# A Fourier-filter and maxout kernel: the opening's row fix, last products, last tile and first transforms rearranged, and one read split

## The chip, the cores and the metric

The kernel runs on one core of a Trainium2 chip. A core has TensorE (matrix products), VectorE, ScalarE and GpSimd (elementwise work), SyncE, which issues transfers here, and 16 DMA engines that all queues share. The metric is the time of one execution on the device in microseconds; smaller is better. Values come from the median of repeated executions; the profile is of one execution.

In the profile's rows PE is TensorE, PEld its weight loads, DVE VectorE, ACT ScalarE, POOL GpSimd and SPq the transfer queue of SyncE. L12 is line 12 of the kernel before.

## The reference

A global filter in the frequency domain along the sequence, and a two-branch maximum network over each token.

```python
# x: (8, 3072, 256); filt_r, filt_i: (1537, 256); w1, w2: (256, 1024); w_out: (1024, 256)
X = np.fft.rfft(x, axis=1)
Y = X * (filt_r + 1j * filt_i)[None, :, :]
y = np.fft.irfft(Y, n=3072, axis=1).reshape(24576, 256)
h = np.maximum(y @ w1, y @ w2)
out = h @ w_out
```

## The kernel before

**The transform.** The 3072 positions are split as 96 x 32. A transform of length 96 (stage 1), one of length 32 with the twiddle factors (stage 2), the product with the filter, and the two inverse stages (3 and 4) are all matrix products with tables of sines that the kernel makes itself. `C1` is the table of stage 1, `U` that of stage 2 (24 units `u` of 64 columns), `VP` and `VQ` those of stage 3, `G1` that of stage 4. `F` holds the filter in 12 x 2 slices. Stages 2, product and 3 run over six pairs of units, `v` = 0 to 5: `s2(b, v)` makes two tiles `px`, `product` makes two tiles `pq` of 128x1024 from them and `F`, and `s3` (for batch 0 `s3t`) makes `pz` from these.

**The network.** `max(a, b) = relu(a - b) + b`, so the kernel takes `Wd = w1 - w2` and `M = w2 @ w_out`. Tokens go in 64 tiles `tt` of 384, eight to a batch: `moe_h(tt, j)` (j = 0 to 7, L476) makes `ph` with `Wd` and ScalarE or VectorE takes its relu into `gt`; `moe_o(tt, ...)` (L519) accumulates `po` from `M` with `y` and from `Wo` with `gt`, and VectorE and a transfer on GpSimd's queue bring it out.

**The order.** Everything runs in the order in which it is written (`manual_schedule`), engine by engine. There are two parts.

*The opening*, L621 to L718, takes batch 0 through its transform on the chip alone, and prepares the weights:

- Tables: `table_c` (L180), `tables_u`, `sines_u`, `table_g` (L251), `table_v` and `put_v` (L256, L273). Stage 1 is `s1t` (L554), its turn is `t1` (L566).
- The filter: GpSimd's queue issues `load_f`; `put_fz` writes 32 rows, `double_f` copies half of `F` (VectorE for the first eight slices, L128), and `fix_f` (L144) writes one row of one slice.
- [...] For v = 5 `shared_product` (L394) gives three quarters of the second one to VectorE and one quarter to GpSimd.
- `s3t(v, pq)` (L577) is 32 products of 64x64 columns into two PSUM tiles, led by products with the constant `W1` (128x512, L581) whose result nobody reads; its two tiles are then written to `zT` by ScalarE, for v = 4 and 5 by ScalarE and VectorE.
- `t2(c, engines)` (L599) turns four of `zT`'s 32 columns back with eight transposes into `pr`, and the engines named copy it to `zr`. `s4(tt)` (L454) makes `y` of a token tile from it and `G1`: two tiles `py`, one evicted by ScalarE, one by VectorE.
- `spin(n)` (L615) is n products with `W1` in between, again unread.
- Behind the products GpSimd's queue does, in this order: `load_x(1, 2, 2)`, `load_wo`, `prep_wd(0)`, two more `load_x`, `prep_wd(1)` to `(3)` (a quarter of `Wd` each, L298), `cast_w2` twice (half of `w2b` each, L291) and `table_ct`. Quarter q of `Wd` serves j = 2q and 2q + 1. `prep_t(0)` (L300) transposes the first half of `w2b`, `prep_m` makes `M`.

*The stream*, L777 on, runs 64 steps per batch, step = 8 i + j. At each step it calls `moe_h`, some of `moe_o` of the tile before, and what the tables `mid` and `todo` hold for that step: the transform of the next batch. For batch 1 that is `f1(1, c)` (L323, c = 0 to 15; the first four stand in the opening): a product with `C1` into `pa`, an eviction to `at` by ScalarE or VectorE, and for each odd c a store to the DRAM tile `ad`. `f1_read(1)` (L340) reads it back as `bt` in three pieces (units 0-4, 4-12, 12-24) at step 13. `visit(1, n)` at steps 25, 28, 31, 35, 38, 42 and 46 does `s3(1, n-1)`, `s2(1, n)`, stage 1 of batch 2 for some quads, and the products. Batch 2's input comes by `load_xf(2, c)` (L91, SyncE's queue, three buffers `XF`) and `fold(2, c)` (GpSimd, L101) at steps listed in `plan_f2`.

[...] A tile that is made waits until the tile that used its bank before has been read.

Of the kernel before, what the change touches and what calls it, by code (L numbers as in the profile page):

```python
# [15 lines left out]
D = 256  # L16
HID = 1024
NP = 96
# [9 lines left out]
def kernel(  # L28
# [115 lines left out]
    def fix_f():  # L144
        V.tensor_copy(F[32:33, 0, 0, 0], FZ[32:33, 0])

# [8 lines left out]
    cid = init.tile([128, 128], FP32)  # L155

    hv = init.tile([128, 2, 1], FP32)
    load_x(0, 0, 1)
# [33 lines left out]

    def table_ct():
# [127 lines left out]
    at_ = {}  # L321

    def f1(b, c, engine):  # L323
# [4 lines left out]
        at = at_[b]  # L328
        pa = ps.tile([96, 2, D], FP32, tag="ps", name="pa")
        TE.matmul(pa, C1, xb[b, c // 2][:, 2 * (c % 2):2 * (c % 2) + 2], start=True, stop=True)  # L330
        o_ = at[0:96, 2 * (c % 4):2 * (c % 4) + 2]
        if engine is V:
            V.tensor_copy(o_, pa)
        else:
            S.activation(o_, pa, AF.Copy)
        if c % 2 == 1:
            m0 = 2 * (c % 4) - 2
            nc.sync.dma_start(out=ad[b][:, 2 * c - 2:2 * c + 2], in_=at[0:96, m0:m0 + 4])

    def f1_read(b):  # L340
        bt[b] = bpool.tile([128, NU, D], BF16, tag="bt", name="bt")
        src = ad[b].rearrange("(u q) m d -> (q m) u d", q=4)
        for u0, u1 in ((0, 4), (4, 12), (12, NU)):
            nc.sync.dma_start(out=bt[b][:, u0:u1], in_=src[:, u0:u1])

# [42 lines left out]
    def product(E, v, s, px, pool=None):  # L388
        pq = (pool or pqpool).tile([128, 2, 2, D], BF16, tag="pq", name="pq")
        E.tensor_tensor(pq, px.rearrange("p (o i) d -> p o i d", o=1).to_broadcast([128, 2, 2, D]),  # L390
                        F[:, :, 2 * v:2 * v + 2, s], OP.mult)
        return pq

    def shared_product(v, s, px, xs_, pool):  # L394
        pq = pool.tile([128, 2, 2, D], BF16, tag="pq", name="pq")
        V.tensor_tensor(pq[:, 0], px, F[:, 0, 2 * v:2 * v + 2, s], OP.mult)
        V.tensor_tensor(pq[:, 1, 0], px[:, 0], F[:, 1, 2 * v, s], OP.mult)
        G.tensor_tensor(pq[:, 1, 1], xs_[:, 1], F[:, 1, 2 * v + 1, s], OP.mult)
        return pq
# [177 lines left out]
    def s3t(v, pq):  # L577
        pool, tag = (ps, "ps") if v % 2 else (pso, "po")
        pz = [pool.tile([128, 2, 2, 2, 2, NM], FP32, tag=tag, name="pt%d" % g) for g in range(2)]
        for _ in range(2 if v == 1 else 1):  # L580
            TE.matmul(pz[0].rearrange("p i s r c m -> p (i s r c m)"), W1[:, 0:128], W1, start=True, stop=True)  # L581
        for i in range(2):
            for s in range(2):
                for dc in range(2):
                    for q, tab in enumerate((VP, VQ)):
                        for g in range(2):
                            TE.matmul(pz[g][:, i, s, :, dc], pq[s][64 * g:64 * g + 64, q, i, 128 * dc:128 * dc + 128],  # L587
                                      tab[64 * g:64 * g + 64, 2 * v + i, s].rearrange("p (r m) -> p r m", r=2),
                                      start=(q == 0), stop=(q == 1))
        zv = zT.rearrange("p c m (w g) q -> p w g (c m) q", g=2)  # L590
        for g in range(2):
            o_ = zv[:, 2 * v:2 * v + 2, g]
            i_ = pz[g].rearrange("p i s r c m -> p i (c m) (s r)")
            if v >= 4 and g == 1:
                V.tensor_copy(o_, i_)
            else:
                S.activation(o_, i_, AF.Copy)

    def t2(c, engines):  # L599
# [3 lines left out]
        for k, engine in enumerate(engines):  # L603
            pr = ps.tile([96, n, D], BF16, tag="ps", name="pr")
            m0 = 4 * c + n * k
            for m in range(n):
                for dc in range(2):
                    TE.transpose(pr[:, m, 128 * dc:128 * dc + 128], zT[:, dc, m0 + m].rearrange("p u q -> p (u q)"),  # L608
                                 I128)
# [29 lines left out]
    bt[0] = bpool.tile([128, NU, D], BF16, tag="bt", name="bt")  # L639
    zT = bpool.tile([128, 2, NM, NU, 4], BF16, tag="bt", name="zT")  # L640
    for n in range(6):
# [44 lines left out]
    pxs[5] = s2(0, 5)  # L686
    stage_x(5)
    for v in (2, 3):
# [140 lines left out]
```

## Time and profile before

| what | value |
|---|---|
| median of 3 runs | 498.68 us (496.98, 498.87, 498.68) |
| the profiled execution | 498.64 us |
| its span, first to last instruction | 496.8 us |
| mean granted TensorE clock | 0.989 |
| busy: TensorE, VectorE, ScalarE, GpSimd | 483.8, 335.4, 320.4, 258.7 us |
| HBM traffic | 203 GB/s over the span |

A row of the timeline gives the start, the time, engine and line, operation, output <- inputs, shapes and the count of instructions merged; in square brackets stands the idle time before it and what ended it. A row of the chain gives start, time, engine, tile and line. A row of stretches gives the stretch, its length, the busy time of PE, PEld, DVE, ACT and POOL with counts (PE alone where it was asked for TensorE), the granted clock, the DMA engines' busy share and GB/s. Ends of matrix products are modelled: they are pipelined, so one of 512 columns shows 0.38 us but the next can start earlier.

### The profile page before, as it was taken

The page shows a single profiled execution, that of the slowest core. Times are in us where ns is not written, and L with a number is a line of the kernel's source. Part 1 is how long each engine was busy: PE and PEld are TensorE (multiplying, and loading weights), DVE is VectorE, ACT ScalarE, POOL GpSimd, SP SyncE. Part 2 cuts the span into 40 slices and gives each one's busy share as a digit, 9 for nine tenths or more (in the row PEclk, how much of TensorE's full clock was granted, in tenths as well). Part 3 has the DMA queues.
Part 4 walks back from the last instruction along what each step waited for, and adds up shares of the span by engine and source line. Part 5 has one row for each costly group of instructions (what it writes and reads, how often), then busy time and mean ns, then how long its engine had stood idle before and what let it go on. Part 6 is the DMA issues. An engine that isn't in the chain of part 4 may idle for free.

```text
span 496.8 us, 14137 instructions
## 1 busy us (share of the span) xinstructions
PE 483.8 (97%) x5759; PEld 353.5 (71%) x5759; DVE 335.4 (68%) x535; ACT 320.4 (64%) x667; POOL 258.7 (52%) x342
## 2 busy tenths in 40 slices
PE   7699999999999999999999999999999999999997
PEld 3457777777777777777777777776777777777775
DVE  7886788468855688467855688457873688556542
ACT  5777478667775677576866668665766656464442
POOL 8694868318466594528646295536842212222220
PEclk9879999999999999999999999999999999999999
DMA  8989988996789867896789977897776834531112
GB/s 128 161 242 224 259 269 260 284 234 190 204 266 221 216 210 223 249 225 174 231 257 227 183 244 211 257 215 168 227 231 175 181 104 129 157 120 66 64 64 86
DMA packets 76626, 97.30 MB, mean 196 GB/s; under 512 B 7985, under 2 KB 54354, under 8 KB 75186
## 3 DMA queue, kind: packets, MB, share of 16 engines
q1 hardware_dynamic: 63218, 66.71, 52.1%
q0 software_dynamic: 13200, 29.60, 21.4%
q8 instruction: 45, 0.74, 0.7%
q14 instruction: 19, 0.16, 0.1%
q10 hardware_dynamic: 144, 0.09, 0.1%
HBM read 53.87 MB, written 47.19 MB: 203 GB/s over the span
## 4 chain that ended last, share of the span: by engine, by line
PE 92%; DMA 3%; ACT 2%; POOL 1%; issue 1%; DVE 0%; SPq 0%; POOLq 0%
PE po L536 34%; PE ph L482 33%; PE po L534 8%; PE pz L408 5%; PE pc L443 3%; PE px L384 2%; PE pa L355 2%; DMA xb<-in_x_dram 2%; DMA zr<-zd 1%; PE pt L587 1%; DMA zd<-zt 1%; PE pr L608 1%; POOL xb L89 1%; PE pt L581 1%; PE pa L330 1%
## 5 line engine op out<-in xcount | busy, mean ns | idle before, releaser
L486 ACT ACTIVATE gt<-ph 128x384 bf16<-128x384 f32 x357 | 175.7, 496 | 138.8 <-PE ph L482 136.2
L536 PE MATMUL po<-Wo,gt 128*128 128x256 bf16 x1528 | 262.7, 273 | 1.2 <-issue 1.2
L536 PEld LDWEIGHTS <-gt 128*128 128x128 bf16 x1528 | 144.7, 98 | 68.1 <-issue 13.5
L495 POOL DMA_DIRECT2D out_dram<-ot x186 | 103.1, 558 | 154.7 <-DVE ot L547 138.7
L390 DVE TENSOR_TENSOR pq<-px,F 128x1024 bf16<-128x1024 f32 x91 | 106.9, 1218 | 25.7 <-PE px L384 25.4
L484 DVE TENSOR_SCALAR gt<-ph 128x384 bf16<-128x384 f32 x155 | 83.6, 551 | 53.5 <-PE ph L482 47.1
L482 PEld LDWEIGHTS <-Wd 128*128 128x128 bf16 x1024 | 99.6, 98 | 13.7 <-issue 0.3
L104 POOL TENSOR_TENSOR xb<-XF 128x512 bf16<-128x512 f32 x48 | 61.3, 1277 | 66.9 <-DMA XF<-in_x_dram 31.7
L547 DVE TENSOR_SCALAR ot<-po 128x512 f32<-128x512 f32 x83 | 57.0, 686 | 35.0 <-PE po L536 33.1
L105 POOL TENSOR_TENSOR xb<-XF 128x512 bf16<-128x512 f32 x48 | 61.1, 1274 | 0.0
L359 ACT ACTIVATE at<-pa 128x512 bf16<-128x512 f32 x96 | 51.8, 611 | 3.4 <-PE pa L355 3.3
L412 ACT ACTIVATE zt<-pz 128x512 bf16<-128x512 f32 x84 | 45.6, 594 | 5.7 <-PE pz L408 1.9
L448 ACT ACTIVATE ce<-pc 128x384 f32<-128x384 f32 x56 | 23.7, 490 | 6.7 <-PE pc L443 6.0
L408 PE MATMUL pz<-pq,VP 64*64 64x256 bf16 x336 | 22.2, 281 | 0.0
L384 PE MATMUL px<-bt,U 64*64 64x256 bf16 x384 | 20.4, 283 | 1.2 <-ACT VQ L279 0.7
L408 PE MATMUL pz<-pq,VQ 64*64 64x256 bf16 x336 | 21.1, 269 | 0.0
L408 PEld LDWEIGHTS <-VP 64*64 64x64 bf16 x336 | 10.0, 105 | 13.3 <-issue 12.7
L355 PE MATMUL pa<-xb,CT 64*64 64x512 bf16 x192 | 18.0, 377 | 0.0
L443 PEld LDWEIGHTS <-zr 48*128 48x128 bf16 x896 | 13.1, 93 | 4.8 <-issue 4.4
L443 PE MATMUL pc<-G,zr 48*128 48x48 bf16 x896 | 15.4, 180 | 0.3 <-DMA zr<-zd 0.3
L384 PEld LDWEIGHTS <-U 64*64 64x64 bf16 x384 | 10.6, 109 | 3.9 <-issue 3.6
L618 PE MATMUL pd<-W 128*128 128x512 bf16 x28 | 9.2, 437 | 1.5 <-DVE zero L150 1.5
(383 smaller groups left out, 632.1 us busy)
## 6 DMA issues: line engine op xcount, KB each, us to landing
out_dram<-ot POOLq DMA_DIRECT2D x186, 128.0 KB, 3.8
XF<-in_x_dram SPq DMA_DIRECT2D x96, 192.0 KB
ad<-at SPq DMA_DIRECT2D x56, 192.0 KB
zd<-zt SPq DMA_DIRECT2D x42, 256.0 KB
zr<-zd SPq DMA_DIRECT2D x56, 192.0 KB
bt<-ad SPq DMA_DIRECT2D x13, 768.0 KB
WS<-in_moe_w_dram SPq DMA_DIRECT2D x4, 512.0 KB
xb<-in_x_dram POOLq DMA_DIRECT2D x8, 192.0 KB, 5.6
```

What stands on the lines that cost most here:

```text
L104: G.tensor_tensor(t_[:, 0], f[:, 0], f[:, 1], OP.add)
L105: G.tensor_tensor(t_[:, 1], f[:, 0], f[:, 1], OP.subtract)
L359: S.activation(at[:, m0:m0 + 2], pa[g], AF.Copy)
L390: E.tensor_tensor(pq, px.rearrange("p (o i) d -> p o i d", o=1).to_broadcast([128, 2, 2, D]), F[:, :, 2 * v:2 * v + 2, s], OP.mult)
L408: TE.matmul(pz[g][64 * s:64 * s + 64, i], tab[64 * g:64 * g + 64, 2 * v + i, s], pq[s][64 * g:64 * g + 64, q, i], start=(q == 0), stop=(q ...
L412: S.activation(zt[:, :, g], pz[g], AF.Copy)
L482: TE.matmul(ph, Wd[:, dc, 128 * j:128 * j + 128], y_[:, dc], start=(dc == 0), stop=(dc == 1))
L484: V.tensor_scalar(gt[tt][:, j], ph, 0.0, None, OP.max)
L486: S.activation(gt[tt][:, j], ph, AF.Relu)
L495: E.dma_start(out=dst, in_=ot[tt // 2][:, 3 * (tt % 2) + c])
L536: TE.matmul(p_, g_[:, n - 2, blk], Wo[:, n - 2], start=(e == 0), stop=(e == 9))
L547: V.tensor_scalar(ot[tt // 2][:, e - 1:e + 1], po[q // 2 % 2], SCALE, None, OP.mult)
```

## The change

- `fix_f` runs on GpSimd in place of VectorE, at the same place of the program.
- `shared_product` and `stage_x(5)` are gone; VectorE makes both products of v = 5 whole.
- `zT` has another order of its axes, in eight groups `o` of four columns. To suit it, `G1` is made from a second sine table `CP`, which holds `C1`'s columns in another order, and `s3t` and `t2` address their tiles accordingly. For v = 5 each of the two PSUM tiles is written to `zT` in two parts: group 0 first, then groups 1 to 7.
- The unread products: `s3t` is led by 3, 4, 2, 2, 3 and 0 of them for v = 0 to 5 (before: 1, 2, 1, 1, 1, 1), and a new function `busy(n)` puts 2 behind each of `s2(0, 1)` and `s2(0, 0)`, 3 behind `table_v(0, 1)`, 9 behind `sines_u(1)` and 2 behind the last `put_v`. They write to a tile of `pso`. The two `spin(1)` ahead of the stream become `fill` of 1, 1 and 2.
- `f1` is cut into `f1_in` (the product) and `f1_out` (eviction and store). The products of c = 0 to 3 of batch 1 stand between the steps of the opening's end; the evictions of c = 0 and 1 come after `s4(0)`, those of c = 2 and 3 at step 0 of the stream.
- In batch 0 the three pieces of `f1_read` are issued at steps 13, 14 and 15; `load_xf(2, 2)` and `(2, 3)` move from steps 10 and 12 to 13 and 14 (behind that step's piece), their folds from 16 and 20 to 19 and 22.

```diff
     def fix_f():
-        V.tensor_copy(F[32:33, 0, 0, 0], FZ[32:33, 0])
+        G.tensor_copy(F[32:33, 0, 0, 0], FZ[32:33, 0])
...
+        S.activation(CP.rearrange("p (g w c) -> p g w c", g=2, c=4),
+                     uc.rearrange("p (w g s) r -> p g w (s r)", g=2, s=2), AF.Sin, bias=zero[0:NP], scale=TWO_PI)
...
-        TE.matmul(pg, C1, I128[0:NP, 0:NP], start=True, stop=True)
+        TE.matmul(pg, CP, I128[0:NP, 0:NP], start=True, stop=True)
...
     def f1(b, c, engine):
+        f1_in(b, c)
+        f1_out(b, c, engine)
+
+    def f1_in(b, c):
+        pas[c] = ps.tile([96, 2, D], FP32, tag="ps", name="pa")
+        TE.matmul(pas[c], C1, xb[b, c // 2][:, 2 * (c % 2):2 * (c % 2) + 2], start=True, stop=True)
+
+    def f1_out(b, c, engine):
...
-    def f1_read(b):
-        bt[b] = bpool.tile([128, NU, D], BF16, tag="bt", name="bt")
+    def f1_read(b, u0, u1):
+        if u0 == 0:
+            bt[b] = bpool.tile([128, NU, D], BF16, tag="bt", name="bt")
         src = ad[b].rearrange("(u q) m d -> (q m) u d", q=4)
-        for u0, u1 in ((0, 4), (4, 12), (12, NU)):
-            nc.sync.dma_start(out=bt[b][:, u0:u1], in_=src[:, u0:u1])
+        nc.sync.dma_start(out=bt[b][:, u0:u1], in_=src[:, u0:u1])
...
     def s3t(v, pq):
...
-        for _ in range(2 if v == 1 else 1):
-            TE.matmul(pz[0].rearrange("p i s r c m -> p (i s r c m)"), W1[:, 0:128], W1, start=True, stop=True)
+        for _ in range((3, 4, 2, 2, 3, 0)[v]):
+            TE.matmul(pz[0].rearrange("p o i s r c m -> p (o i s r c m)"), W1[:, 0:128], W1, start=True, stop=True)
...
-        for g in range(2):
-            o_ = zv[:, 2 * v:2 * v + 2, g]
-            i_ = pz[g].rearrange("p i s r c m -> p i (c m) (s r)")
-            if v >= 4 and g == 1:
-                V.tensor_copy(o_, i_)
-            else:
-                S.activation(o_, i_, AF.Copy)
+        for o0, o1 in ((0, 1), (1, 8)) if v == 5 else ((0, 8),):
+            for g in range(2):
+                o_ = zT[:, o0:o1, :, :, g, 2 * v:2 * v + 2].rearrange("p o c m w q -> p o (c m) (w q)")
+                i_ = pz[g][:, o0:o1].rearrange("p o i s r c m -> p o (c m) (i s r)")
+                if v >= 4 and g == 1:
+                    V.tensor_copy(o_, i_)
+                else:
+                    S.activation(o_, i_, AF.Copy)
...
     def products(v):
         pool = pq0 if v > 2 else pqpool
         pq = [product(V, v, 0, pxs[v][0], pool)]
-        if v == 5:
-            pq.append(shared_product(v, 1, pxs[v][1], xs[v], pool))
-        else:
-            pq.append(product(G, v, 1, xs[v], pool) if v in POOLED else product(V, v, 1, pxs[v][1], pool))
+        pq.append(product(G, v, 1, xs[v], pool) if v in POOLED else product(V, v, 1, pxs[v][1], pool))
         return pq

+    def busy(n):
+        pd = pso.tile([128, 512], FP32, tag="po", name="pd")
+        for _ in range(n):
+            TE.matmul(pd, W1[:, 0:128], W1, start=True, stop=True)
+
     pqs = {}
-    pxs = {v: s2(0, v) for v in (1, 0)}
+    pxs = {}
+    for v in (1, 0):
+        pxs[v] = s2(0, v)
+        busy(2)
     stage_x(0)
     put_v(0, 1, table_v(0, 1))
+    busy(3)
     pxs[2] = s2(0, 2)
     stage_x(2)
     sines_u(1)
+    busy(9)
     put_v(1, 0, table_v(1, 0))
     pxs[3] = s2(0, 3)
     stage_x(3)
     put_v(1, 1, table_v(1, 1))
+    busy(2)
...
     pxs[5] = s2(0, 5)
-    stage_x(5)
...
-    f1(1, 0, S)
-    spin(1)
+    f1_in(1, 0)
+    fill(1)
     t2(0, (V, S))
-    f1(1, 1, V)
-    spin(1)
+    f1_in(1, 1)
+    f1_in(1, 2)
+    fill(1)
     s4(0)
-    f1(1, 2, S)
-    f1(1, 3, V)
+    f1_in(1, 3)
+    f1_out(1, 0, S)
+    f1_out(1, 1, V)
+    fill(2)
...
-        plan(b, read, f1_read, nb)
+        for k, (u0, u1) in enumerate(((0, 4), (4, 12), (12, NU))):
+            plan(b, read + k, f1_read, nb, u0, u1)
...
+    plan(0, 0, f1_out, 1, 2, S)
+    plan(0, 0, f1_out, 1, 3, V)
     plan_f1(0, 1, (5, 6, 7, 7, 9, 9, 10, 10, 11, 11, 12, 12), 13)
     plan_f2(0, (25, 28, 31, 35, 38, 42, 46), ((0,), (), (1,), (2,), (3,), (4,), (5, 6)),
-            (8, 8, 10, 12, 17, 20, 24, 28), (10, 13, 16, 20, 24, 27, 30, 33))
+            (8, 8, 13, 14, 17, 20, 24, 28), (10, 13, 19, 22, 24, 27, 30, 33))
```

More of the change, by code (lines that the diff above doesn't have):

```diff
@@ L155 @@
     cid = init.tile([128, 128], FP32)
+    CP = init.tile([NP, 96], BF16)
     hv = init.tile([128, 2, 1], FP32)
@@ L321 @@
     at_ = {}
+    pas = {}
     def f1(b, c, engine):
+        f1_in(b, c)
[4 more added lines that the diff above has]
+    def f1_out(b, c, engine):
         if c == 0:
@@ L327, in f1 @@
             at_[b] = apool.tile([128, 8, D], BF16, tag="at", name="at")
-        at = at_[b]
-        pa = ps.tile([96, 2, D], FP32, tag="ps", name="pa")
-        TE.matmul(pa, C1, xb[b, c // 2][:, 2 * (c % 2):2 * (c % 2) + 2], start=True, stop=True)
+        at, pa = at_[b], pas.pop(c)
         o_ = at[0:96, 2 * (c % 4):2 * (c % 4) + 2]
@@ L391, in product @@
                         F[:, :, 2 * v:2 * v + 2, s], OP.mult)
[L392 to L398, printed above, removed]
         return pq
@@ L578, in s3t @@
         pool, tag = (ps, "ps") if v % 2 else (pso, "po")
-        pz = [pool.tile([128, 2, 2, 2, 2, NM], FP32, tag=tag, name="pt%d" % g) for g in range(2)]
-        for _ in range(2 if v == 1 else 1):
-            TE.matmul(pz[0].rearrange("p i s r c m -> p (i s r c m)"), W1[:, 0:128], W1, start=True, stop=True)
+        pz = [pool.tile([128, 8, 2, 2, 2, 2, 4], FP32, tag=tag, name="pt%d" % g) for g in range(2)]
+        for _ in range((3, 4, 2, 2, 3, 0)[v]):
+            TE.matmul(pz[0].rearrange("p o i s r c m -> p (o i s r c m)"), W1[:, 0:128], W1, start=True, stop=True)
         for i in range(2):
@@ L586, in s3t @@
                         for g in range(2):
[L587 to L588 removed]
+                            TE.matmul(pz[g][:, :, i, s, :, dc].rearrange("p o r m -> p r o m"),
+                                      pq[s][64 * g:64 * g + 64, q, i, 128 * dc:128 * dc + 128],
+                                      tab[64 * g:64 * g + 64, 2 * v + i, s].rearrange("p (r o m) -> p r o m", r=2, m=4),
                                       start=(q == 0), stop=(q == 1))
[L590 to L597 removed]
+        for o0, o1 in ((0, 1), (1, 8)) if v == 5 else ((0, 8),):
[6 more added lines that the diff above has]
+                    S.activation(o_, i_, AF.Copy)
     def t2(c, engines):
@@ L607, in t2 @@
                 for dc in range(2):
-                    TE.transpose(pr[:, m, 128 * dc:128 * dc + 128], zT[:, dc, m0 + m].rearrange("p u q -> p (u q)"),
+                    TE.transpose(pr[:, m, 128 * dc:128 * dc + 128],
+                                 zT[:, (m0 + m) // 4, dc, (m0 + m) % 4].rearrange("p g w q -> p (g w q)"),
                                  I128)
@@ L639 @@
     bt[0] = bpool.tile([128, NU, D], BF16, tag="bt", name="bt")
-    zT = bpool.tile([128, 2, NM, NU, 4], BF16, tag="bt", name="zT")
+    zT = bpool.tile([128, 8, 2, 4, 2, NW, 4], BF16, tag="bt", name="zT")
     for n in range(6):
@@ L710, with fill @@
     gpool = ctx.enter_context(tc.tile_pool(name="gpool", bufs=2))
-    f1(1, 0, S)
-    spin(1)
+    pd = pso.tile([128, 512], FP32, tag="po", name="pd")
+    def fill(n):
+        for _ in range(n):
+            TE.matmul(pd, W1[:, 0:128], W1, start=True, stop=True)
+    f1_in(1, 0)
+    fill(1)
     t2(0, (V, S))
-    f1(1, 1, V)
-    spin(1)
+    f1_in(1, 1)
+    f1_in(1, 2)
+    fill(1)
     s4(0)
-    f1(1, 2, S)
-    f1(1, 3, V)
+    f1_in(1, 3)
+    f1_out(1, 0, S)
+    f1_out(1, 1, V)
+    fill(2)
     todo = {}
```

## The prediction

> **What bounds the kernel now.** I read the page first, then the busy time by stretches, the chain of waits, and the timeline of each engine for the first 66 us, where every edit lies. PE is TensorE, DVE VectorE, ACT ScalarE, POOL GpSimd.
>
> ```profile
> PE 483.8 (97%) x5759; PEld 353.5 (71%) x5759; DVE 335.4 (68%) x535; ACT 320.4 (64%) x667; POOL 258.7 (52%) x342
> ...
> 38.00:45.00 7.00, 7.00 (x77) 5.27 (x76) 6.10 (x11) 5.56 (x11) 5.08 (x8) 1.00 1.13 206
> 38.00:98.50 60.50, 60.50 (x660) 45.09 (x660) 43.40 (x65) 41.58 (x86) 39.65 (x46) 1.00 0.93 260
> ```
>
> TensorE is busy in every microsecond from 38 to 98.5 (the busy time behind the stretch's length), and for 97% of the whole span. Whatever the opening saves reaches the end only if this stream starts earlier and still finds its inputs. The stream's first product is at 37.73. So two questions decide: by how much does 37.73 move, and what then arrives too late?
>
> The opening's own limit is in the chain of waits:
>
> ```profile
> 26.04 0.97 PE pt L581 x2
> ...
> 28.54 0.54 PE pt L581
> 29.08 1.01 PE pt L587 x30
> 30.10 0.59 ACT zT L597
> ...
> 33.22 0.58 PE pt L587 x32
> 34.11 0.62 PE pt L587 x32
> 34.76 0.70 DVE zT L595
> 35.59 0.63 PE pr L608 x8
> ```
>
> One `s3t` takes 1.01 us early and 0.58 us late, because the clock differs. I laid windows of 3.41 us on the clock's edges (the last three columns: clock, DMA share, GB/s):
>
> ```profile
> 7.64:11.05 3.41, 2.62 (x27) 1.00 1.05 172
> ...
> 17.88:21.29 3.41, 2.31 (x95) 1.00 0.92 123
> 21.29:24.70 3.41, 1.39 (x39) 0.50 0.70 146
> 24.70:28.12 3.42, 3.12 (x93) 0.50 0.56 165
> 28.12:31.53 3.41, 3.30 (x62) 0.50 1.06 289
> 31.53:34.94 3.41, 3.41 (x131) 1.00 1.03 321
> ```
>
> The half clock lasts 10.24 us, three such windows. It begins behind a window with 2.31 us of busy TensorE, while 2.62 had kept the full clock.
>
> **The change, part by part.** First the row fix and the last product pair:
>
> ```profile
> 18.11 0.49 POOL L122 DMA_DIRECT2D F<-in_filt_r_dram  x1 [0.34 <-DMA F<-in_filt_r_dram]
> ...
> 19.82 2.40 POOL L122 DMA_DIRECT2D F<-in_filt_i_dram  x2
> 23.43 2.12 POOL L390 TENSOR_TENSOR pq<-xs,F 128x1024 bf16<-128x1024 f32 x1 [1.20 <-DVE F L128]
> ...
> 26.07 6.30 POOL L390 TENSOR_TENSOR pq<-xs,F 128x1024 bf16<-128x1024 f32 x3
> 32.34 0.66 POOL L398 TENSOR_TENSOR pq<-xs,F 128x256 bf16<-128x256 f32 x1
> 32.95 0.56 POOL L89 DMA_DIRECT2D xb<-in_x_dram  x1
> 33.51 0.93 POOL L294 DMA_DIRECT2D Wo<-in_moe_w_out_dram  x1
> ...
> 36.72 3.74 POOL L298 TENSOR_TENSOR Wd<-WS 128x512 bf16<-128x512 f32 x3
> 40.40 2.01 POOL L291 CAST w2b<-WS 128x1024 bf16<-128x1024 f32 x2
> ```
>
> ```profile
> 18.49 4.76 DVE L128 COPY F<-F 32x4096 bf16<-32x4096 bf16 x4
> 23.28 0.28 DVE L145 CAST F<-XF 1x256 bf16<-1x256 f32 x1
> 23.76 8.13 DVE L390 TENSOR_TENSOR pq<-px,F 128x1024 bf16<-128x1024 f32 x7 [0.19 <-DVE F L145]
> ...
> 32.40 0.41 DVE L397 TENSOR_TENSOR pq<-px,F 128x256 bf16<-128x256 f32 x1
> ```
>
> ```profile
> L142 POOL CAST F<-XF x2: 520/562/605, 7.6 to 8.2; 32x256 bf16<-32x256 f32 x2
> ```
>
> VectorE loses the fix, so its products start at 23.28 and not 23.76; eight whole ones at 8.13/7 = 1.16 us end at 23.28 + 9.29 = 32.57. Before, the shared form ended at 32.81. Gain there: 0.24.
>
> GpSimd loses the shared quarter: 32.95 - 32.34 = 0.61 us. It gains the fix, 0.56 us by L142 (same 256 columns). It can start when the last filter issue ends, 22.22, inside an idle stretch that ends at 23.43: bound 0 us. If it has to let VectorE's copies end first (18.49 + 4.76 = 23.25), it ends at 23.81 and delays the first product by 0.38 (0.42 with L142's longest). I take 0.38: the two issues at 19.82 took 1.20 each where the one at 18.11 took 0.49, and 1.20 is the pitch of VectorE's copies (4.76/4 = 1.19), so GpSimd's work under these copies ends with them. Behind the fix stand all of GpSimd's products, loads and weight preparations. Everything from L89 at 32.95 on therefore moves earlier by 0.61 - 0.38 = 0.23 us (bounds 0.19 and 0.61).
>
> [...]
>
> The fills on TensorE: `busy` puts 2, 2, 3, 9 and 2 products of 512 columns into the stretches 18 to 26, and `s3t` goes from 1, 2, 1, 1, 1, 1 to 3, 4, 2, 2, 3, 0 (v = 0 to 5). Their aim shows in the windows: 17.88 to 21.29 rises from 2.31 by up to the seven short fills, above 2.62, and the clock should stay at 1.00 until 38. At full clock a fill costs at most 0.90 - 0.58 = 0.32 (the pitch 33.22 to 34.11 less one `s3t`). The last two reuse a buffer of the second VQ table, so they wait until ScalarE has evicted it; behind them stand `s3t(1)` and `s2(4)`, which VectorE needs for its sixth product at 23.28 + 5 x 1.16 = 29.1. `s2(4)` ended at 28.54; four more fills at 0.32 add 1.3, and the full clock takes off 0.43 (one `s3t`) and 0.33 (two fills at 0.32 for 0.97): 29.1, just in time.
>
> `s3t(4)` cannot end before GpSimd's last product, 32.37 + 0.38 = 32.75. With two `s3t` of 0.58 that gives 33.9, or 34.2 where the three fills are still in the way; I take 34.05. Before it was 34.11 + 0.62 = 34.73, so 0.68 is gained. The last tile's first part has an eighth of the columns: between 0.28 us (L145) and 0.70 (the whole tile); I take 0.3, as it is small, and gain 0.4. The second part then sits on ScalarE and VectorE ahead of the evictions of `t2(0)`, but their inputs need another 0.63 us on TensorE (L608), which covers it. The early `f1_in` and late `f1_out` move the four evictions (0.6 to 0.7 us each) behind the first `y`; nothing waits for them before step 4. Sum: the first product of the stream comes 0.68 + 0.4 = 1.1 us earlier, at about 36.6 (bounds 0.5 and 1.4). The second sine table, the order of `zT` and `G1`, and `stage_x(5)` dropped are ScalarE work with gaps around it: 0.
>
> Now what it meets:
>
> ```profile
> 37.73 0.89 PE L482 MATMUL ph<-y__998,Wd 128*128 128x384 bf16 x4
> ...
> 40.77 0.49 PE L482 MATMUL ph<-y__998,Wd 128*128 128x384 bf16 x2
> ...
> 41.64 0.61 PE L305 MATMUL pt<-I,w2b 128*128 128x128 bf16 x8
> ...
> 44.19 0.60 PE L536 MATMUL po<-Wo,gt 128*128 128x256 bf16 x4
> ```
>
> ```profile
> DMA to landing us min/median/max: 10.6/10.6/10.6
> ```
>
> (the last is the one transfer of Wo, L294.) The product at 40.77 needs the last quarter of Wd, ready at 36.72 + 3.74 = 40.46: slack 0.31. The transposes at 41.64 need the first half of w2b, ready at 40.40 + 2.01/2 = 41.41: slack 0.23. The product at 44.19 needs Wo, landed at 33.51 + 10.6 = 44.1: slack 0.1. None of these moves with TensorE; all move with GpSimd, by 0.23. So TensorE starts 1.1 early, waits, and is ahead by at most 0.54 at 40.77, 0.46 at 41.64 and 0.33 at 44.19. From there on it is dense. **Gain: 0.3 us.** Bounds: 0.1 (Wo lands no earlier, since the DMA engines are loaded: share 1.13 in 38 to 45) and 0.7 (0.61 + 0.1).
>
> Batch 0's read in pieces:
>
> ```profile
> 57.57 1.96 SPq L344 DMA_DIRECT2D bt<-ad  x3
> ...
> 65.05 0.41 PE L384 MATMUL px<-bt,U 64*64 64x256 bf16 x8
> ...
> 57.50:64.50 7.00, 7.00 (x77) 5.10 (x73) 5.25 (x8) 4.87 (x10) 6.97 (x9) 1.00 0.90 259
> ```
>
> The second piece now stands on SP behind the XF load of tile 2, and the third behind tile 3; both loads come later and leave the stores ahead of them alone. From 57.57, piece one (0.26 MB), that load (0.52 MB) and piece two (0.52 MB) are 1.3 MB; at the 259 GB/s of this stretch 5.0 us, so it lands at 62.6, before 65.05 - 0.3. Cost 0, and nothing to gain, as TensorE waited for nothing here. If the cover is gone, `s2(1,1)` and all behind it wait. Loads 5 and 6 of XF now wait for later folds, and behind them on SP stands the first store of `zd` (step 28), which is read back from step 39 on.
>
> **The sum.** The profiled execution took 498.64 us, span 496.8, so 1.8 lies around it; it agrees with the median of the three runs, 498.68. 498.64 - 0.3 = **498.3 us**.
>
> **The rivals.** *The whole opening arrives.* If GpSimd's chain were not the gate, all 1.1 would stay: 497.5. For it: POOL has idle time ahead of 23.43. Against it: three separate due times with slacks of 0.1 to 0.31. *Nothing arrives*: Wo lands where it did, 498.5.
>
> *The clock stays at half and the fills cost.* Place: TensorE from 26 to 34.7. At half clock a fill takes 0.49 (0.97 for two); two more in `busy`, two more in `s3t(1)` are 1.9 us before `s2(4)`, and five net ones follow at 0.32 (1.6 us). Against that, `s3t(0)` slips behind 31.53 and saves 0.4, and TensorE had a wait of 0.6 to spare (L597 at 30.10). `s3t(5)` ends 2.5 late; the split gives back 0.4: the stream starts 2.1 late with nothing left to absorb it, 498.64 + 2.1 = 500.7. It decides if the window 17.88 to 21.29 stays under about 2.6 us busy. For it: 3.12 us in 24.70 to 28.12 did not bring the full clock back, and where the windows fall may differ by execution. Against it: the fills close most of the 1.1 us of gaps there.
>
> [...]
>
> *Piece two comes late*: at 150 GB/s instead of 259, 1.3 MB take 8.7 us, to 66.3, 1.5 after its due time: 498.3 + 1.5 = 499.8. Against it: the rate of the row above, with the same kinds of transfer in it.
>
> **The numbers.** Forecast 0.57, whole opening 0.13, nothing arrives 0.11, half clock 0.10, late piece 0.06, something else 0.03. The runs before spread from 496.98 to 498.87; one row may tell why:
>
> ```profile
> 336.35 0.28 PE L536 MATMUL po<-Wo,gt 128*128 128x256 bf16 x1 [1.23 <-issue]
> ```
>
> This stop has no cause in the trace; an execution without it would be 1.2 us shorter. So the range goes from 498.3 - 0.5 - 1.2 = 496.6 up to 499.8, short of the half-clock case. [...] Faster 0.05 (a median without the stop and with the whole opening), slower 0.05, same 0.90.
>
> **What would show it.** Right: clock 1.00 from 18 to 38; first GpSimd product at 23.8; first stream product near 36.6; TensorE idle 0.3 to 0.8 us in all ahead of Wd, w2b or Wo between 38 and 44; L536 first at 43.9. Wrong: L536 first near 43.1, clock 0.50 anywhere after 21, TensorE idle at bt near 65, or a span over 498.

## The result and the profile after

| | before | changed |
|---|---|---|
| median | 498.10 us (22 runs, 496.63 to 499.04) | **499.14 us** (22 runs, 497.37 to 503.12) |
| profiled execution | 498.64 us, span 496.8 | 503.12 us, span 501.3 |
| ratio to before | | **1.003** (95%: 1.0019 to 1.0041) |

The changed kernel is slower by 1.04 us where 0.3 us of gain was forecast. Two more measurements of the same kernel gave 1.004 (1.001 to 1.007) and 1.0035 (1.0018 to 1.0052). The profiled execution is the longest of its 22: what it shows is real, but larger than in most. Line numbers are now the changed kernel's: L672 is `busy`, L585 the unread products of `s3t`, L591 its own products, L395 `s2`, L401 `product`, L658 ScalarE's copies of `px` to `xs`, from which GpSimd's products are made, L602 and L600 the copies to `zT`, L486 `moe_h`, L540 `moe_o`.

**The clock.** Stretches, TensorE only: length, PE busy, granted clock, DMA share, GB/s. First the kernel before, then the changed one.

```profile
18.00:38.00 20.00, 16.00 (x419) 0.74 0.87 203
38.00:98.50 60.50, 60.50 (x660) 1.00 0.93 260
98.50:125.00 26.50, 26.50 (x337) 1.00 0.89 214
318.00:345.00 27.00, 25.50 (x291) 1.00 0.90 198
```

```profile
18.00:38.00 20.00, 17.93 (x438) 1.00 0.84 201
38.00:98.50 60.50, 60.29 (x656) 1.00 0.93 235
98.50:125.00 26.50, 24.22 (x286) 0.94 0.89 212
318.00:345.00 27.00, 27.00 (x311) 1.00 1.00 238
```

The unread products did hold the full clock through the opening (1.00 for 0.74). The loss is 2.28 us of idle TensorE and a stretch of half clock between 98.5 and 125. The last row holds a gain that the forecast had only as an end of its range: the stop near 335 is gone.

**The opening.** Timelines of the changed kernel: TensorE (rows of the second tables and of `s3t`'s own products left out, but one), VectorE, GpSimd.

```profile
22.56 2.12 PE L672 MATMUL pd<-W 128*128 128x512 bf16 x9
...
27.27 0.59 PE L672 MATMUL pd<-W 128*128 128x512 bf16 x2 [0.67 <-ACT VQ L282]
27.70 1.02 PE L585 MATMUL pt<-W 128*128 128x512 bf16 x4
28.66 0.20 PE L591 MATMUL pt<-VP,pq 64*128 64x64 bf16 x2
...
29.23 0.29 PE L395 MATMUL px<-bt,U 64*64 64x256 bf16 x1
29.98 0.41 PE L395 MATMUL px<-bt,U 64*64 64x256 bf16 x7 [0.46 <-ACT zT L602]
30.32 0.82 PE L585 MATMUL pt<-W 128*128 128x512 bf16 x3
...
31.64 0.41 PE L395 MATMUL px<-bt,U 64*64 64x256 bf16 x8
```

```profile
23.67 5.75 DVE L401 TENSOR_TENSOR pq<-px,F 128x1024 bf16<-128x1024 f32 x5
30.42 1.22 DVE L401 TENSOR_TENSOR pq<-px,F 128x1024 bf16<-128x1024 f32 x1 [1.00 <-DMA xb<-in_x_dram]
32.10 2.36 DVE L401 TENSOR_TENSOR pq<-px,F 128x1024 bf16<-128x1024 f32 x2 [0.46 <-PE px L395]
```

```profile
20.14 2.41 POOL L122 DMA_DIRECT2D F<-in_filt_i_dram  x2
22.59 1.23 POOL L145 CAST F<-XF 1x256 bf16<-1x256 f32 x1
23.91 2.13 POOL L401 TENSOR_TENSOR pq<-xs,F 128x1024 bf16<-128x1024 f32 x1
...
31.13 2.13 POOL L401 TENSOR_TENSOR pq<-xs,F 128x1024 bf16<-128x1024 f32 x1 [0.36 <-ACT xs L658]
```

The last two of `busy` wait 0.67 us for ScalarE, four more follow, and `s3t(1)` begins its own work only at 28.66. Behind it `s2(4)` starts at 29.23, but its second product runs only at 29.98, right behind ScalarE's first copy to `zT` (0.46 us of idle time, 0.75 us between two products that stand 0.003 us apart in the kernel before), and it ends at 30.39. Why `s2(4)` has to wait for that copy the rows don't say. VectorE's sixth product starts at 30.42: that is its true releaser, though the bracket names a transfer long done. Its seventh starts at 32.10, right behind `s2(5)` (31.64 + 0.41). VectorE, which was to run without a break to 32.57, ends at 34.46.

**Batch 0.** Timelines of the changed kernel: SyncE's queue, then TensorE at the read-back of `zd`; last the same queue in the kernel before.

```profile
62.65 9.43 SPq L94 DMA_DIRECT2D XF<-in_x_dram  x6
72.12 0.43 SPq L417 DMA_DIRECT2D zd<-zt  x1
...
93.71 4.62 SPq L387 DMA_DIRECT2D zr<-zd  x4
...
99.42 3.10 SPq L387 DMA_DIRECT2D zr<-zd  x2
```

```profile
101.27 0.18 PE L447 MATMUL pc<-G,zr 48*128 48x48 bf16 x1 [0.61 <-DMA zr<-zd]
103.11 1.12 PE L447 MATMUL pc<-G,zr 48*128 48x48 bf16 x47 [1.66 <-DMA zr<-zd]
```

```profile
59.64 5.13 SPq L94 DMA_DIRECT2D XF<-in_x_dram  x6
66.39 0.38 SPq L413 DMA_DIRECT2D zd<-zt  x1
...
89.56 3.24 SPq L376 DMA_DIRECT2D zr<-zd  x4
93.86 1.62 SPq L376 DMA_DIRECT2D zr<-zd  x2
```

Six load issues hold the queue for 9.43 us in place of 5.13, the store of `zd` behind them starts 5.73 us later, and the last `zr` reads are issued 5.56 us later, while the stream itself was only some 2 us late. TensorE waits for them 0.61 + 1.66 us, and a window at half clock follows (103.0 to 106.4). The trace shows the chain: `load_xf(2, 2)` and `(2, 3)` now stand behind the read's first and second piece and are issued from 58.22 on (before: 51.01 to 55.27), their folds start at 64.69 and 68.77 (before: 57.56 and 61.13) behind idle waits of 4.67 and 1.59 us for these loads, and the six issues wait for the folds.

```profile
64.69 1.26 POOL L104 TENSOR_TENSOR xb<-XF 128x512 bf16<-128x512 f32 x1 [4.67 <-DMA XF<-in_x_dram]
...
68.77 1.27 POOL L104 TENSOR_TENSOR xb<-XF 128x512 bf16<-128x512 f32 x1 [1.59 <-DMA XF<-in_x_dram]
```

**The ledger.** Start of the same `ph` product in the two traces: the first 37.73 to 39.25 (+1.52, of which 0.31 is there at the first transpose of stage 1), the 17th 42.97 to 44.83 (+1.86), the 121st +2.11, the 161st, behind the `zr` wait and the half clock, +6.04; then two stops that only the kernel before has, near 326 and 335, take back 1.8, a wait for `zr` near 388 that only the changed kernel has loses 0.4, and the last `ph` product is at 493.72 for 489.23 (+4.49).

### The profile page after: what moved, and what is told of

Read it like the earlier page. It is cut to its first block, busy times and chain, and to the rows that moved or that the text cites. A ratio compares the mean times of both kernels' runs of the same rounds, so it can differ in the third digit from the quotient of the medians.

```text
span 501.3 us, 14191 instructions
## 1 busy us (share of the span) xinstructions
PE 489.8 (98%) x5786; PEld 356.1 (71%) x5786; DVE 335.3 (67%) x534; ACT 320.4 (64%) x668; POOL 258.8 (52%) x342
## 4 chain that ended last, share of the span: by engine, by line
PE 90%; DMA 5%; ACT 1%; POOL 1%; DVE 1%; SPq 0%; issue 0%; POOLq 0%; DVEq 0%; ACTq 0%
PE po L540 33%; PE ph L486 31%; PE po L538 8%; PE pz L412 5%; PE pc L447 3%; DMA zr<-zd 2%; PE px L395 2%; PE pa L366 2%; DMA xb<-in_x_dram 2%; DMA zd<-zt 1%; PE pd L672 1%; POOL xb L89 1%; PE pt L585 1%; PE pt L591 1%; PE pa L334 1%; ACT at L370 1%
## 5 line engine op out<-in xcount | busy, mean ns | idle before, releaser
L540 PE MATMUL po<-Wo,gt 128*128 128x256 bf16 x1528 | 263.2, 273 | 0.0
L540 PEld LDWEIGHTS <-gt 128*128 128x128 bf16 x1528 | 144.9, 98 | 67.1 <-issue 12.5
L401 DVE TENSOR_TENSOR pq<-px,F 128x1024 bf16<-128x1024 f32 x92 | 108.2, 1218 | 27.2 <-PE px L395 25.9
L486 PEld LDWEIGHTS <-Wd 128*128 128x128 bf16 x1024 | 99.8, 98 | 14.0 <-issue 0.2
L395 PE MATMUL px<-bt,U 64*64 64x256 bf16 x384 | 19.9, 272 | 0.5 <-ACT zT L602 0.5
L395 PEld LDWEIGHTS <-U 64*64 64x64 bf16 x384 | 10.4, 106 | 4.1 <-issue 4.0
L549 DVE COPY ot<-po 128x512 f32<-128x512 f32 x12 | 8.2, 684 | 4.2 <-PE po L540 4.2
```

Of the source, the lines that this page charges most:

```text
L486: TE.matmul(ph, Wd[:, dc, 128 * j:128 * j + 128], y_[:, dc], start=(dc == 0), stop=(dc == 1))
L540: TE.matmul(p_, g_[:, n - 2, blk], Wo[:, n - 2], start=(e == 0), stop=(e == 9))
```

## The experiments

Two loss sites, so the question was which of them the medians carry, and what in each. The theories, by the letters that the expectations use: **A**: the unread products stand on TensorE's path and delay `s2(4)`, `s2(5)` and with them VectorE. **B**: the later loads and folds hold SyncE's queue, so that `zd` and `zr` come late. **C**: the moved `f1` evictions and the divided last tile cost by themselves. **D**: the full clock is worth more than the unread products cost. **E**: the read of `bt` in three pieces is late by itself. **F**: the stop near 335 depends only on how many instructions stand ahead of it. **G**: the unread products cost only together with the rest of the new opening.

"Opening" below is the time from the first transpose of stage 1 to the start of the stream's 17th `ph` product, "stream" from there to the last `ph` product, both from the profiled execution. The first loses what happens ahead of the transposes, which differs by up to 1.4 us between executions. Openings with a star hold a wait of 2.2 to 4.1 us of VectorE for the second half of the filter, which landed late in those executions.

| run | median us | before, same chip | ratio (95%) | opening | stream |
|---|---|---|---|---|---|
| before | 498.10 | | | 27.83 | 446.26 |
| changed | 499.14 | 498.10 | 1.003 (1.0019 to 1.0041) | 29.38 | 448.89 |
| changed, 2nd | 499.45 | 498.04 | 1.004 (1.001 to 1.007) | 30.34* | 448.58 |
| changed, 3rd | 498.95 | 497.77 | 1.0035 (1.0018 to 1.0052) | 29.43 | 445.63 |
| batch 0 undone | 498.38 | 497.98 | 1.0007 (0.9996 to 1.0018) | 29.18 | 444.47 |
| the same, 2nd | 498.47 | 497.77 | 1.0015 (1.0002 to 1.0028) | 29.22 | 444.79 |
| pieces kept | 498.62 | 498.04 | 1.0012 (0.9995 to 1.0029) | 29.41 | 444.34 |
| batch 0 alone | 498.51 | 497.98 | 1.0009 (0.9996 to 1.0022) | 27.97 | 446.06 |
| late unread ones out | 497.58 | 497.98 | 0.9994 (0.9976 to 1.0011) | 28.45 | 444.62 |
| unread ones as before | 498.66 | 497.98 | 1.0016 (0.9996 to 1.0036) | 29.32* | 445.17 |
| unread ones in waits | **497.14** | 498.04 | 0.9986 (0.9966 to 1.0005) | 28.11 | 444.40 |
| fewer, one eviction later | **497.14** | 498.12 | 0.9984 (0.9964 to 1.0004) | 27.69 | 445.39 |
| unread ones in before | 497.85 | 498.12 | 0.9994 (0.9978 to 1.0011) | 29.13* | 444.37 |
| before, 28 more products | 498.24 | 498.04 | 1.0003 (0.9983 to 1.0023) | 29.77* | 444.30 |

### Batch 0: undone, alone, and its two halves apart

Undone, in the changed kernel (and in the next four experiments on the opening too):

```diff
-            plan(b, read + k, f1_read, nb, u0, u1)
+            plan(b, read, f1_read, nb, u0, u1)
...
-            (8, 8, 13, 14, 17, 20, 24, 28), (10, 13, 19, 22, 24, 27, 30, 33))
+            (8, 8, 10, 12, 17, 20, 24, 28), (10, 13, 16, 20, 24, 27, 30, 33))
```

> The opening as changed; the read in one step and the loads and folds of batch 0 as before the change. Theory A (the unread products stand on TensorE's path in the opening): the first ph stays at 39.0 to 39.3 us, and the time stays 1.0 us over before (ratio 1.002). Theory B (the loads and folds moved in batch 0 make zr of batch 1 late): the long executions above 500.5 us vanish, TensorE no longer waits for zr near 100 us, and if B were all, the ratio is 1.000.

Alone: the kernel before with this edit the other way round.

> The kernel before with only the read in pieces and the moved loads and folds. Theory A: ratio 1.000, first ph at 37.7. Theory B: the last zr read of batch 1 is issued near 98 us where it was at 93.9, TensorE waits 0.5 to 2.5 us for it near 99 in some executions, ratio 1.001 to 1.003 with a tail above 500 us.

Pieces kept: the changed kernel with the second line of the diff only (loads and folds back, reads still at steps 13, 14 and 15).

> The changed kernel with the loads and folds of tiles 2 and 3 back at steps 10, 12, 16 and 20; the read stays in three steps. Theory B (SP's queue stands behind folds that became later, and with it the zd stores and zr reads): the last zr read is issued no later than 1.5 us after its place of before relative to the first ph, no wait for zr near 100, ratio to before as with all of batch 0 undone, 1.0007 +- 0.001. Rival E (the read in pieces itself is late): the wait near 100 stays, ratio 1.002 or more.

Beside this one the changed kernel ran again on the same chip:

> The changed kernel itself once more, for a second profile. Theory B: TensorE waits 0.4 us or more for zr near 100 us here too, the last zr read of batch 1 is issued on SP 60 us or more after the first ph (before: 93.9 - 37.7 = 56.1). If the wait of the first profile was an accident: no wait over 0.2 us there.

And last both kernels in five rounds on one chip:

> The changed kernel once more, five rounds, on one chip with the same kernel less its batch 0 edit (next run). B (later loads and folds make batch 2's zr late): median 0.8 to 1.1 us above the next run's, and its slowest executions 502 or more. A (unread products on TensorE's path in the opening make up nearly all of the loss): within 0.4 us of the next run's.

> The changed opening with the loads, folds and reads of batch 0 where they were. B: 0.8 to 1.1 us below the changed kernel, no execution above 501; against the kernel before +0.3 to +0.6 us if the unread products' path (A) costs too, within 0.3 of it if the opening as a whole costs nothing. A alone: +0.8 or more against the kernel before.

With the loads and folds back TensorE waits for no `zr` near 100 us in any of the seven traces of the changed opening that have them so; with the later ones it does in all four: 2.27, 1.14 and 0.99 us in the changed kernel, 0.25 with batch 0 alone. SyncE's queue with the pieces kept, as one of them:

```profile
61.40 5.12 SPq L94 DMA_DIRECT2D XF<-in_x_dram  x6
69.11 0.38 SPq L417 DMA_DIRECT2D zd<-zt  x1
...
91.54 3.40 SPq L387 DMA_DIRECT2D zr<-zd  x4
96.01 2.32 SPq L387 DMA_DIRECT2D zr<-zd  x2
```

The six issues take 5.12 us again, and B names the cause. E is not tested by itself: with the loads back at steps 10 and 12 the three pieces stand in the queue one behind the other again (59.74, 1.57 us for all three). B's size is less than it expected (0.8 to 1.1 us, ratio 1.001 to 1.003 with batch 0 alone). The changed kernel lies above its neighbour without the later folds by 499.45 - 498.62 = 0.83 us and by 498.95 - 498.47 = 0.48 us; batch 0 alone costs 498.51 - 497.98 = 0.53, which its own interval doesn't tell from none. All three point one way: 0.5 to 0.8 us in the median, with ratios to the kernel before whose intervals overlap. The upper end carries more: the changed kernel's longest executions are 503.12, 505.47 and 502.6 us, those of the same opening without the later folds 499.17, 500.56 and 500.32 (the kernel before reached 501.2 in one set). Counted from the stream's 17th `ph` product, the last `zr` read is issued after 50.9 us before, 50.3 to 52.0 in the seven traces with the loads and folds back, 53.5 with batch 0 alone, and 54.6, 55.0 and 53.3 in the changed kernel's three. Whether the new opening makes it later still can't be told from these.

### The opening: the unread products taken out, put back, moved

Late ones out: none in `s3t`, and not the last `busy(2)`.

```diff
-        for _ in range((3, 4, 2, 2, 3, 0)[v]):
+        for _ in range((0, 0, 0, 0, 0, 0)[v]):
...
-    busy(2)
```

> The opening as changed with batch 0 undone, and no unread products behind the last put_v and in s3t (those of 2, 2, 3 and 9 stay). Theory A: VectorE's eight products run without a gap and end near 32.9, the first ph comes at 36.5 to 37.2, and the stream is ahead of before by 0.2 to 0.6 us at po, held back by Wd, w2b or Wo; ratio 0.999. Rival C (the late evictions of f1 or the split tile cost the time, not the unread products): first ph no earlier than 38.5, ratio at least 1.001.

As before: no `busy` at all, `s3t` with 1, 2, 1, 1, 1, 1.

> The opening as changed with batch 0 undone, and the unread products as before the change (none of 2, 2, 3, 9 and 2; s3t with 1, 2, 1, 1, 1, 1). Theory A: the clock falls to half near 21 and comes back near 31.5, the first ph comes at 36.8 to 37.5, ratio 0.999 to 1.000. Rival D (the full clock is worth more than the products cost): first ph later than 38, ratio over 1.001. Rival C as for the kernel without late unread products.

In waits: the last `busy(2)` moves from ahead of `s3t(1)` to ahead of `s2(4)`, into the wait seen there; `s3t(1)` has none. In all there are six unread products fewer.

```diff
-        for _ in range((3, 4, 2, 2, 3, 0)[v]):
+        for _ in range((1, 0, 2, 2, 5, 0)[v]):
...
-    busy(9)
+    busy(7)
...
-    busy(2)
     for v in (1, 0, 2):
...
     s3t(1, pqs[1])
+    busy(2)
     pxs[4] = s2(0, 4)
```

> The opening as changed with batch 0 undone, and the unread products put where TensorE waits anyway: 7 in place of 9 behind sines_u(1), none behind the last put_v, 2 between s3t(1) and s2(4), and s3t led by 1, 0, 2, 2, 5, 0. Theory A (unread products ahead of work that VectorE or the tile needs cost their own time; in waits they only hold the clock): clock 1.00 from 8 us to the end, VectorE's eight products end near 32.7, first ph at 36.4 to 37.0, first po at 43.7 to 44.1, ratio 0.996 to 0.998 with a spread under 1.5 us. Rival C (other parts of the opening cost the time): first ph no earlier than 38, ratio 1.000 or more.

Fewer, and one eviction later: as the last, but 2 for `s3t(4)` in place of 5 (nine fewer than in the changed kernel), and

```diff
-    plan(0, 0, f1_out, 1, 3, V)
+    plan(0, 2, f1_out, 1, 3, V)
```

> The kernel with unread products in waits, with s3t(4) led by 2 in place of 5 of them and the eviction of f1's c = 3 at step 2 in place of 0. Theory A: s3t(4) starts its own products behind GpSimd's last product (32.4 to 32.7) and not at 33.6, the first ph comes 0.5 to 0.7 us earlier than with 5 (36.8 to 37.1), and the 0.35 us in which TensorE waits for zr's copy near 40 goes; the stream is then held by Wd and w2b, so the step from first ph to the 16th token product grows. Ratio to before 0.996 to 0.998.

The other way round, the changed kernel's `busy` and `s3t` counts in the kernel before, with nothing else changed:

> The kernel before with the changed kernel's unread products alone (2, 2, 3, 9, 2 and s3t with 3, 4, 2, 2, 3, 0). Theory A (they stand on TensorE's path): clock 1.00 from 8 us on, VectorE has gaps of 0.4 to 1.1 us ahead of its sixth and seventh product, first ph at 38.7 to 39.4 (before: 37.7), ratio 1.001 to 1.003. Rival G (they cost only together with the new zT layout or the late evictions): first ph at 37.0 to 37.8, ratio 0.999 or less.

In the kernel before with these products, `s2(4)`, and then VectorE's products behind the filter wait:

```profile
29.54 0.41 PE L384 MATMUL px<-bt,U 64*64 64x256 bf16 x8
```

```profile
32.52 2.36 DVE L390 TENSOR_TENSOR pq<-px,F 128x1024 bf16<-128x1024 f32 x2 [2.22 <-DMA F<-F]
```

The opening without the batch 0 edit lies above the kernel before by 0.40 and 0.70 us, the second clear of none. With the unread products rearranged the median goes from 498.38 to 497.14: 1.24 us, though no part of the computation changed. (These runs were on different chips; against the kernel before on the same chip it is +0.40 to -0.90 and -0.98.) Timelines of the last version (fewer, one eviction later), TensorE, then VectorE:

```profile
26.08 0.38 PE L672 MATMUL pd<-W 128*128 128x512 bf16 x1
26.60 0.76 PE L395 MATMUL px<-bt,U 64*64 64x256 bf16 x8
...
36.15 0.86 PE L486 MATMUL ph<-y__1015,Wd 128*128 128x384 bf16 x4
...
39.05 0.50 PE L486 MATMUL ph<-y__1015,Wd 128*128 128x384 bf16 x2 [0.87 <-POOL Wd L301]
...
43.81 0.60 PE L540 MATMUL po<-Wo,gt 128*128 128x256 bf16 x4
```

```profile
23.12 9.14 DVE L401 TENSOR_TENSOR pq<-px,F 128x1024 bf16<-128x1024 f32 x8
```

`s2(4)` now starts at 26.60, VectorE's eight products run without a break to 32.26, the stream starts at 36.15, and TensorE then waits for `Wd`: the opening that was forecast, held at `Wd` as was forecast. The quarter of `Wd` that it waits for had itself stood 0.43 us for a transfer:

```profile
37.73 2.49 POOL L301 TENSOR_TENSOR Wd<-WS 128x512 bf16<-128x512 f32 x2 [0.43 <-DMA WS<-in_moe_w_dram]
```

So the place of the unread products decides in the changed opening. But A is only part of it. The same products in the kernel before cost nothing in the median (497.85 for 498.12), a ratio of 0.9994, where A expected 1.001 to 1.003 and G 0.999 or less. The filter wait of VectorE in that trace hides what they do to the stream's start; what they do to TensorE can be read: `s2(4)` runs in one piece there. Counted from the first transpose of stage 1 it ends after 13.40 us in the kernel before (13.03 with batch 0 alone, the same opening), after 13.98 with these products, and after 14.74 to 14.93 in the six executions with the changed opening as it is. So the products cost some 0.6 to 0.95 us, and the 0.75 us between the first and the second product of `s2(4)` come on top. That gap is in all ten traces of the new opening (0.2 to 0.9 us, and 0.75 also with the unread products of before), its end 0.05 us behind ScalarE's first copy to `zT` each time, and in none of the four of the old one. It belongs to the rest of the new opening, as G has it; which part brings it was not tried. Where the unread products stand in it, it comes early enough that VectorE doesn't notice.

In the variant with five unread products ahead of `s3t(4)`, VectorE ends at 32.55 as well, but the first stream product is at 37.49 (36.4 to 37.0 was expected); that difference of 1.34 us did not reach the median (497.14 both). At the first `po` with `Wo` 0.47 us of it is left (44.28 and 43.81): the gate takes the rest; and the trace of the version with fewer loses 1.1 us, more than it was ahead, at a wait for `zr` near 383 (0.83 us) that the other doesn't have. Since products were taken out as well as moved, the shares are not told apart. Both ratios are nearer to 1 than the 0.996 to 0.998 expected.

D is not borne out for the late products: without them the trace has half clock from 30.1 to 37.0, and yet the median is 0.8 us under that of the full clock with all of them on the path. But these executions spread from 496.07 to 499.58, too far to make the 0.8 certain, and the first `ph` was at 38.17, later than the 36.5 to 37.2 that A expected. With the unread products of before the result is the one that D expected and A did not: 498.66, the first `ph` at 39.18, half clock from 24.8 to 35.1. But VectorE waits 2.73 us for the filter in that trace, so it doesn't tell them apart. C is not needed: the evictions and the divided tile are in all of these versions.

### The stop near 335

In the kernel before, 28 unread products of 128 columns ahead of the stream:

```diff
         if c < 7:
             spin(2)
+            pd = ps.tile([128, 128], FP32, tag="ps", name="pd")
+            for _ in range(4):
+                TE.matmul(pd, W1[:, 0:128], W1[:, 0:128], start=True, stop=True)
```

> The kernel before with 28 unread products of 128 columns in the first 14 us, where TensorE waits for x; nothing else. Theory F (the stop of TensorE near 335 comes from an instruction block that is fetched too late, and where the block's edge falls depends on the count of instructions ahead of it; this change hides 0.9 to 1.4 us of loss by moving that edge): no stop over 0.2 us near 335, first ph at 37.7 to 38.2, ratio 0.997 to 0.999. If the stop has another cause: it stays at 0.9 to 1.4 us, ratio 1.000.

```profile
318.00:345.00 27.00, 27.00 (x302) 1.00 0.91 214
```

(stretches of that kernel.) The stop is gone from the trace, as F expects, with nothing near it changed. The time is not what F expected (0.997 to 0.999): the opening became 1.9 us longer, with 2.5 us of VectorE's wait for the filter in it, the stream 1.96 us shorter, and the median moved by 0.20 us. Whether the stop is as long in executions that are not profiled can't be read from this.

## Why the prediction was wrong, step by step

- **The row fix: right.** Forecast 23.8 for GpSimd's first product, measured 23.91; the fix took 1.23 us, started under VectorE's copies and ended at 23.82, 0.25 us behind the last of them (23.57). In two other executions (the changed kernel's second, and the counts of before), where GpSimd's last filter issue ended after the copies, it took 0.39. The rows agree with the prediction's estimate that GpSimd's work under these copies ends with them.
- **The clock: right in the opening.** 1.00 from 18 to 38. The half-clock rival did not occur; the half clock at 103 has another cause, the wait for `zr`.
- **`s2(4)` "just in time" at 29.1: the step that failed.** It ended at 30.39. The prediction charged four more unread products at 0.32 and took 0.76 off for the full clock, +0.56 in all. That term was about right: alone in the kernel before, the unread products move the end of `s2(4)` by 0.58 us (0.95 against the other trace of that opening). The wait of 0.67 us for ScalarE's eviction of the second VQ table, which it had named, is in that, and the charge was ample (the six from 27.27 to 28.66, 0.23 us each). What it put at nothing was the rest of the new opening ("ScalarE work with gaps around it: 0"). That brought the 0.75 us in which `s2(4)` stands behind ScalarE's first copy to `zT`. Another 0.31 of the 1.29 is there at the first transpose already.
- **VectorE until 32.57, the last `s3t` done at 34.05 (the prediction calls it `s3t(4)`; its sum goes to the end of `s3t(5)`), stream at 36.6: wrong in consequence.** 34.46, 36.46 and 39.25. The prediction took the two engines' ends as independent; `px` ties them.
- **The gate at `Wd`, `w2b` and `Wo`: right in part, and not reached by the changed kernel.** Forecast for the first `po` with `Wo` 43.9; 43.81 in the version with fewer unread products (0.24 of the 0.38 to 44.19 is there at the first transpose), 46.05 in the changed kernel. Of the three due times only that of `Wd` shows a wait, 0.87 us, and half of it (0.43) comes from a transfer that the prediction did not have.
- **Evictions behind `s4(0)` at nothing: nearly.** TensorE waits 0.19 us ahead of `s4(1)`'s products at 41.73 for the `zr` copy, which VectorE does behind two `f1` evictions. With one of them moved this wait is not there.
- **Batch 0 at 0: wrong.** The place was in the text (loads 5 and 6 behind later folds, the first `zd` store behind them), without a price. It is 0.5 to 0.8 us in the median and 2.3 us of waits, with the half clock behind them, in the profiled execution. The rival that was priced, piece two of `bt` late, did not occur.
- **The sum.** Forecast -0.3, measured +1.04. Of the 1.34 between them some 0.85 is the opening (+0.40 and +0.70 in place of -0.3) and 0.5 to 0.8 batch 0. The rival on the slower side had the right place (unread products between 26 and 34.7) tied to the wrong condition: the delay came at full clock. The measured 499.14 lies inside the stated range of 496.6 to 499.8, but by luck: its upper end stood for the late piece of `bt`, which did not occur.
- **What stays open.** In the traces the changed opening is longer by 1.35 to 1.6 us (29.18 to 29.43 for 27.83), and the stream without the later folds shorter by 1.5 to 1.9, because the stops are gone: about nothing in sum, where the medians show +0.4 to +0.7. Either the stops are shorter in most executions, or the opening's loss is larger; no run tells these apart. Open too is which part of the new opening makes `s2(4)` wait for the copy to `zT`.

## What to carry to other kernels

An unread product that keeps the clock up stands in TensorE's order like any other. Here the six from 27.27 to 28.66 took 0.23 us each, behind a wait of 0.67 us for their own buffer; in the kernel before all of them together moved the end of `s2(4)`, which is written behind them, by 0.58 to 0.95 us. Where the next product had slack this cost nothing in the median (the kernel before with all of them: 497.85 us for 498.12); where another part of the same change used the slack up, as the 0.75 us ahead of `s2(4)` did, it was paid (498.38 us, and 497.14 with the unread products rearranged). Put such products where the trace shows TensorE waiting, with their buffer already free, and check the start of the next product that another engine needs. A part put at 0 because its work is small can still hold up another engine; look for the wait first. Where a load's release moves to a later step, follow the issuing queue to the store behind it and that store's reader, and put a price on it; a risk that is only named counts as zero in the sum.

The versions with the unread products in the waits and batch 0 undone are the best seen here: 497.14 us twice. They lie clearly under the changed kernel; against the kernel before their ratios, 0.9986 and 0.9984, have intervals that just include 1.

## What was unexpected in the hardware

**A stop that goes with the number of instructions ahead of it.** 1.23 us, put down to "issue", a microsecond behind a burst of 48 short `pc` products at 333.42. Three of the fourteen traces have it: before (1.23 us), batch 0 alone (0.85, the same instructions) and the unread products of before (0.69, two matrix products more ahead of it). With 11 more (late unread ones out) and with 28 more it is gone. A later start alone does not remove it: the stream with 0.69 us of it starts 1.45 us later than the kernel before's. The queue of kind "instruction" moves a packet of 16 KB near it. In the three traces with the stop this packet starts between 0.8 us ahead of the burst and 0.1 us behind its start, and TensorE goes on 1.35 to 1.6 us behind the packet's end; in the eleven others it starts 2.1 to 6.6 us ahead of the burst. That TensorE had used up its instructions there would fit, but no run shows it.

**The granted clock does not follow PE's busy time as the profile shows it.** Windows on the grid of the clock's edges, for the changed kernel:

```profile
21.08:24.50 3.42, 3.35 (x31) 1.00 0.82 165
24.50:27.91 3.41, 2.20 (x84) 1.00 0.44 66
27.91:31.33 3.42, 2.96 (x65) 1.00 0.95 238
...
99.59:103.00 3.41, 1.25 (x10) 1.00 0.98 279
103.00:106.42 3.42, 3.31 (x57) 0.50 0.75 254
```

2.20 us busy kept the full clock here, where 2.31 lost it in the kernel before; 1.25 lost it. The prediction's bound of "about 2.6" was no bound. The stretches at half clock are multiples of 3.41 us: one such step in the changed kernel (103.00 to 106.42), three in the kernel before (10.24 us), two without the late unread products (30.14 to 36.96) and three with the unread products of before (24.83 to 35.07). In steps of 3.41 us their starts in the opening, 21.29, 30.14 and 24.83, do not fall on one grid. A grid that falls differently in each execution would also fit the spread of the kernel that leaves gaps (496.07 to 499.58 us without the late unread products, 497.79 to 499.17 with them), but no run shows that it is the cause.

**The second half of the filter lands late in some executions.** VectorE then waits 2.2 to 4.1 us ahead of its sixth product, in four of the profiled executions, with old and new openings alike; GpSimd's product from the same half starts within 0.01 us of it each time (33.37 for both in the changed kernel's second). It is a part of the spread between runs (of the changed kernel's profiled executions the second has 4.10 us of it, the first none), and it blurs two experiments on the opening.
